# Expert 0's input: the last two chunks' rows picked by one-hot products, the other rows read early

## The chip, the cores and the metric

The kernel runs on one core of a Trainium2 chip. The metric is the device time of one execution in microseconds (us); every position in this text is counted from the start of the span of one profiled execution. The engines are PE (TensorE: matmuls and transposes, with its weight loads), DVE (VectorE), ACT (ScalarE), POOL (GpSimd) and SP (SyncE, which here only issues DMAs, in order). Each engine works through its own list in program order.

## The reference, cut to what matters

Three stages follow each other. A recurrence over 768 steps (2 batches, 8 heads, 48 x 48 states) gives `y`; a mixture of 8 experts, of which each token takes one, works on the 1536 tokens of width 384; a gated product works on its result.

```python
x = y.transpose(0, 2, 1, 3).reshape(1536, 384)
logits = x @ w_gate                       # 8 experts
expert_idx = argmax(logits, axis=1)
for i in range(1536):                     # place of a token in its expert's list
    e = expert_idx[i]
    if counts[e] < capacity:
        disp[e, counts[e]] = x[i]; pos[i] = counts[e]; counts[e] += 1; keep[i] = True
h = maximum(einsum('ecd,edf->ecf', disp, w1), 0)      # 384 -> 1024
y = einsum('ecf,efd->ecd', h, w2)                     # 1024 -> 384
out[i] = gate_w[i] * y[expert_idx[i], pos[i]]         # for kept tokens
result = ((out @ w_a) * (out @ w_b)) @ w_out          # 384 -> 1536 -> 384
```

## The kernel before

The order of all instructions is the order in which the Python code emits them (`manual_schedule`); nothing is moved by a scheduler. Waits follow from data and from buffers that are used again. Four parts stand one behind the other.

**Running products.** 96 steps of a scan on DVE, with norms on ACT; the change does not touch them.

**Chunks** (`for c in range(NC)`, 8 chunks of 96 steps, both batches at once). For a chunk, `scores` and `state_mm`/`state_dve` are followed by `outputs(c, b)`, which leaves `y` for batch `b`. `route_a` turns it into token rows `Ys[c]` (96 tokens x 384) and logits `LT`; `route_b` picks the expert (`OH`, a one-hot of 8) and adds to the running counts `EX`; `route_c` ranks the tokens by small products with a triangle and with ones, adds 1536 x expert, and has the slot of every token in `SLU`. Two indirect DMAs of POOL per chunk then write the 96 rows of a batch to their slots in `xs`, a table in DRAM of 8 x 1536 rows that was filled with zeros where experts read (`SLOT` = 240 rows each). The routing of a chunk runs one or two chunks behind; in the last pass (`c == 7`) chunks 5, 6 and 7 are ranked one after the other, chunk 7 one batch at a time.

**Experts.** 32 passes `i` = (expert `e`, quarter `fp`). `load_x(e)` reads 240 rows of `xs` into `R` (SP's queue); it waits for the scatters. `expert_x(e)` transposes them on PE and splits them into a rounded part (ACT) and a rest (DVE), the tile `XTT`. `hmm` has 18 matmuls per pass, `ymm` 18 more, one pass later. In a pass stand also: `wsplit(e + 1, fp)`, a quarter of the next expert's weights into a rounded part (ACT) and a rest (DVE, tile `whl`); `hl`, the rest of the hidden layer (DVE). Weights come by `wload` in 1.5 MB pieces into two buffers (tag `S`), so a piece can be loaded when the splits of the piece two before it are done. The table `UE` says in which expert a unit `n` of the third stage's weights is converted (`raw_load`, `conv_tt`, five DVE operations into a tile `cvt`); `store()` writes finished units to DRAM, in the first pass of the next expert that has units, right behind `wload(e + 1, 1)` on SP. `R`, `hh`, `hl`, `raw` and `cvt` share the nine buffers of tag `T`, and PSUM's tag `h` has three buffers.

Ahead of the first pass the split of the third and fourth quarter of expert 0's weights runs side by side with `tables()` (prefix sums of the counts and the table that takes a slot back to its token). 16 matmuls on ones (`busy`) stand on PE ahead of `expert_x(0)`; nothing reads their result.

**Gated product.** Weights converted while it runs, then rows scattered to the output. It is not touched.

Of the kernel before, what the change touches and what calls it, by code (L numbers as in the profile page):

```python
# [7 lines left out]
I32 = mybir.dt.int32  # L8
# [32 lines left out]
def body(tc, q, k, v, a_re, a_im, w_gate, w1, w2, cap, w_a, w_b, w_o, out, dbg=None):  # L41
# [59 lines left out]
    off_i = cpool.tile([1, E], I32, name="off_i")  # L101
    flag_i = cpool.tile([1, 1], I32, name="flag_i")

    xs = dp.tile([E * NT, DM], F32, name="xs")
    meta = dp.tile([NT, 2], I32, name="meta")
    wf = dp.tile([3, 128, DF], F32, name="wf")
    kid = dp.tile([CH, 128, GD], F32, name="kid")
# [272 lines left out]
    def run(g):  # L380
        for _ in g:
            pass
# [34 lines left out]
    for p in range(NP):  # L417
        if p == 2:
            zt = tT([SP, CU2], F32, "zt")
            V.memset(zt, 0.0)  # L420
            zfill = nc.gpsimd.dma_start(xs.rearrange("(a r) d -> a r d", a=E)[:, :SLOT].rearrange("a (p r) d -> p a (r d)", p=SP), zt.unsqueeze(1).to_broadcast([SP, 8, CU2]))

        if 0 < p < NP - 2:
            load_a(p + 2)
        if p < NP - 1:
            load_k(p)
        gens = []
        load_q(p)
        if p > 0:
            kinv_pre(p - 1, 1)  # L430
        if p + 1 < NP:
            if p == 0:
                gens.append(iter(range(8)))
            if p > 1:
                gens.append(qmul(p - 2))
            gens.append(norm_dve(p + 1))
        else:
            gens.append(qmul(p - 2))
            gens.append(iter(range(8)))
            KL[p] = KLb[p % 2]  # L440
            kl = tT([128, WP], F32, "kl")
            nc.sync.dma_start(kl, lrow(k, p * JP))
            lq = [tT([128, 16 * D], F32, f"last{i}") for i in range(4)]
            last = [kinv_last(8 * h, 8 * h + 8, lq[2 * h], lq[2 * h + 1], kl[:, h * 8 * D:(h + 1) * 8 * D]) for h in range(2)]
        if p > 0:
            if p < NP - 1:
                gens.append(iter(range(4 if p == 1 else 0)))
            gens.append(kinv_dve(p - 1))
        if p == NP - 1:
            QT = [tH([GD, 64, CH], F32, "QT0"), None]  # L450
        bg = chain(*gens)
        for i in range(JP):
            cm = cum(p * JP + i)
            next(cm)
            if p > 0 or i > 3:
                next(bg, None)
            next(cm)
            if p == 0 and i < 4:
                if i == 3:
                    for _ in range(3):  # L460
                        next(first[1])
                    V.tensor_add(g_t, *nx_t[1])
                    run(first[1])
                    norm_pre(1)
                    load_a(2)
                continue
            next(bg, None)
            if p > 0 and i == 2:
                kinv_exp(p - 1)
            if p > 1 and i == (4 if p < NP - 1 else 4):  # L470
                kinv_post(p - 2)
            if p == 0 and i == 5:
                norm_sq(2)
            if p == 0 and i == 9:
                m2_t = tT([128, JP * D], F32, "m2_t")
                V.tensor_add(m2_t, *nx_t[0])
            if i == (6 if p > 0 else 9) and p + 2 < NP:
                norm_pre(p + 2, m2_t)
            if i == 10 and p < NP - 1:
                kinv_pre(p, 0)  # L480
            if p == NP - 1:
                if i == 11:
                    QT[1] = tH([GD, 64, CH], F32, "QT1")
                for ii, pp, hf in CUTS:
                    if ii == i:
                        half(pp, hf)
            if p == NP - 1 and i == 9:
                bg = chain(bg, zip2(last[0], qmul(p - 1)))
            if p == NP - 1 and i == 13:
                kinv_post(p - 1)  # L490
        if p < NP - 1:
            run(bg)
# [167 lines left out]
    def route_c(c, b0=0, b1=B):  # L660
# [15 lines left out]
        pm = cpool.tile([CH, B], F32, tag="pm", name="slot", bufs=2)  # L676
        V.tensor_reduce(pm[:, :n], pri[:, :n], AX.X, ALU.add)
        yield
        V.tensor_copy(SLU[:, t2], pm[:, :n])
        for b in range(b0, b1):  # L680
            i = G.indirect_dma_start(out=xs[:], out_offset=bass.IndirectOffsetOnAxis(ap=SLU[:, B * c + b:B * c + b + 1], axis=0), in_=Ys[c][:, b].rearrange("t p d -> t (p d)"), in_offset=None)
            apart(i, xs_sc)
            after(i, [zfill])
            xs_sc.append(i)
            G.memset(gap_t, 0.0)
# [107 lines left out]
            V.tensor_tensor(lo, t, hi.bitcast(F32), ALU.subtract)  # L793
            yield

    xTs = {}
    cv = tS([128, 2, 4 * CU], I32, "cv0")
    u0 = units[0]
    NU0 = 3
# [5 lines left out]
    for c in range(NC):  # L805
# [5 lines left out]
        if c < NC - 1:  # L811
            scores(c + 1, 0)
            scores(c + 1, 1)
            next(st, None)
            if c > 0:
                route_a(c - 1)
            scores(c + 1, 2)
            scores(c + 1, 3)
            if c == NC - 2:
                run(st)  # L820
            run(zip2(route_b(c - 1) if c > 0 else iter(()), st))
            outputs(c, 0)
            if c + 1 < NC - 1:
                state_mm(c + 1, 0)
            outputs(c, 1)
        else:
            outputs(c, 0)
            run(route_c(c - 2))
            route_a(c - 1)
            run(route_b(c - 1))  # L830
            outputs(c, 1)
            run(route_c(c - 1))
            route_a(c, 0, 1)
            run(route_b(c, 0, 1))
            route_a(c, 1, 2)
            run(zip2(route_b(c, 1, 2), route_c(c, 0, 1)))
            run(route_c(c, 1, 2))
        if c + 1 < NC - 1:
            if c > 3:
                run(route_c(c - 1))  # L840
            state_mm(c + 1, 1)
# [19 lines left out]
        yield from conv_g(u0[n][0], 0, u0[n][1], x[:, :CU], x[:, CU:])  # L861
        conv_out(*u0[n], x[:, CU:].bitcast(F32))

    raw_load(NU0)
    V.tensor_tensor(EX[:, NC], EX[:, NC - 1], OH[:, NTAU - B:], ALU.add)
    tq.release()
    hp.release()

# [8 lines left out]
    for d in range(KD):  # L877
        for i in range(2):
            G.memset(x2[d][i].bitcast(F32), 0.0)
    XT, Hp, yps = {}, {}, {}  # L880
    offs = {}

    sel = xpool.tile([CH, NTAU, E], F32, name="sel")
# [82 lines left out]
        V.tensor_tensor(flag_i, nm[:, 0:1], nm[:, 1:2], ALU.max)  # L966
        yield

    Rt = {}

    def load_x(e):
        R = Rt[e] = tT([SP, 2, DM], F32, f"R{e}")
        after(nc.sync.dma_start(R, xs[e * NT:e * NT + SLOT].rearrange("(a p) d -> p a d", p=SP)), xs_sc)

    def expert_x(e):
        R = Rt[e]
        xp = [pse([128, KD, SP], f"xp{e}_{a}", f"xp{a}", 1) for a in range(2)]
# [42 lines left out]

    seq = [(e, fp) for e in range(E) for fp in range(4)]

    UE = {0: (3,), 1: (4, 5), 2: (6, 7), 3: (8,), 4: (9,), 5: (10,), 6: (11,)}
    load_x(0)
    wload(1, 0)
    side = chain(wsplit_g(0, 2, 4), wsplit_g(0, 3, 4))
    tb = tables()
    run(zip2(side, (next(tb) for _ in range(7))))


    busy = pse([128, 512], "busy", "y0", 1)
    for _ in range(16):
        PE.matmul(busy, ones_b, ones_b.unsqueeze(1).to_broadcast([128, 4, 128]), start=True, stop=True)
    XTT = tC([128, 2, 2, KD, SLOT], F32R, "XTT")
    expert_x(0)
    YPS = [pse([128, 2, SLOT], f"yps{d}", f"y{d}", 1) for d in range(KD)]
    def load_off(e):
        offs[e] = nc.values_load(off_i[:, e:e + 1], engines=[mybir.EngineType.Activation, mybir.EngineType.DVE], min_val=0, max_val=NT, skip_runtime_bounds_check_because="exclusive prefix sums of counts that add up to NT")
# [1 line left out]
    for i, (e, fp) in enumerate(seq):  # L1040
# [8 lines left out]
            m2load(i - 26)  # L1049
        hmm(e, fp)  # L1050
        if i == 0:
            next(tb)
        if i == 6:
            run(tb)
        if fp == 2:
# [17 lines left out]
            next(cg)  # L1073
        elif us and fp == 3:
            run(cg)
        if e + 1 < E:
            wsplit(e + 1, fp)
        elif fp < 2:
            m2split(fp)
# [257 lines left out]
```

## Time and profile before

| | |
|---|---|
| median of 3 runs | 619.63 us (617.08 to 622.54) |
| the profiled execution | 618.06 us, span 616.4 us |
| busy share of the span | PE 84%, DVE 71%, ACT 45%, POOL 13% |
| mean granted TensorE clock | 0.929 |
| chain that ended last | PE 63%, DVE 24%, DMA 6%, ACT 3% |

The shares are averages over stages with different limits. The chain of waits says, followed back from the last instruction, what each step waited for; it is read here for the stretch from the last chunk (from 212 us) to the fifth expert (326 us). Behind 326 us PE is busy without a gap until the last rows are written. [...]

### The profile page before, as it was taken

Reading aid. Unit: us, or ns where it says so; the run is one execution under the profiler, and the core shown is the slowest. Engines: PE = TensorE matmul, PEld = TensorE weight load, DVE = VectorE, ACT = ScalarE, POOL = GpSimd, SP = SyncE. Lnnn points to the kernel's source line nnn. Section 1 sums busy time; section 2 is a strip of 40 time slices with the busy share of each in tenths; the row PEclk is TensorE's granted clock in tenths of the full one; section 3 lists DMA queues with packets and bytes.
Section 4 is the critical chain, followed back from the end, with each engine's and each line's share of the span. In section 5 each row is a group of like instructions: output and inputs, shape, how many; then the busy total and the mean of one; then the engine's idle time right before and its main releaser. Section 6 shows DMA issues by size and latency. Waiting matters only on the chain.

```text
span 616.4 us, 10343 instructions
## 1 busy us (share of the span) xinstructions
PE 519.3 (84%) x4021; PEld 463.1 (75%) x4021; DVE 436.3 (71%) x951; ACT 276.1 (45%) x481; POOL 79.6 (13%) x127
## 2 busy tenths in 40 slices
PE   0064745789899888987999999999999999999993
PEld 0022422689889758987899999888888888888992
DVE  5899999975998853896688774766676777623331
ACT  5656563683435434553566563353443333211220
POOL 2000000040224273011221200000000000002121
PEclk9987677769999877997999999999999999999997
DMA  4148743289965127758578744121212121001010
GB/s 149 55 141 219 222 114 85 60 152 221 223 191 206 46 70 242 233 190 281 177 254 247 236 159 127 52 78 51 78 52 77 53 77 53 1 2 52 23 54 30
DMA packets 62945, 77.56 MB, mean 126 GB/s; under 512 B 29416, under 2 KB 52584, under 8 KB 62888
## 3 DMA queue, kind: packets, MB, share of 16 engines
q1 hardware_dynamic: 60040, 68.75, 37.8%
q0 software_dynamic: 2576, 7.68, 4.4%
q8 instruction: 33, 0.54, 0.4%
q10 hardware_dynamic: 272, 0.39, 0.2%
q14 instruction: 24, 0.20, 0.1%
HBM read 61.27 MB, written 15.54 MB: 125 GB/s over the span
## 4 chain that ended last, share of the span: by engine, by line
PE 63%; DVE 24%; DMA 6%; ACT 3%; issue 2%; SPq 0%; POOL 0%; POOLq 0%; DVEq 0%; ACTq 0%
PE ab L1102 24%; PE o L1118 12%; PE yps L1015 9%; PE h L999 8%; DVE t L271 4%; DVE A L273 3%; DMA wf<-cvt 2%; PE sc L581 2%; DVE KL L336 2%; PE l L299 1%; DMA temps<-in_a_re_dram 1%; DVE whl L711 1%; PE U L550 1%; PE xt L636 1%; DVE A L377 1%
## 5 line engine op out<-in xcount | busy, mean ns | idle before, releaser
L1102 PE MATMUL ab<-x2h,m2h 128*128 128x512 f32 (+1 forms) x480 | 142.1, 369 | 0.0
L1102 PEld LDWEIGHTS ab<-x2h,m2h 128*128 128x128 f32 x480 | 87.4, 188 | 14.4
L1102 PE MATMUL ab<-x2l,m2h 128*128 128x512 f32 (+1 forms) x240 | 88.8, 370 | 0.0
L311 PE MATMUL n<-temps,ident 128*128 128x384 f32 x40 | 27.9, 869 | 54.5 <-ACT temps L308 54.5
L1118 PE MATMUL o<-m2h,gh 128*128 128x384 f32 x288 | 73.6, 336 | 0.0
L999 PE MATMUL h<-XTT,whl 128*128 128x240 f32 x576 | 73.0, 282 | 0.5 <-ACT XTT L987 0.5
L1015 PE MATMUL yps<-hh,whl 128*128 128x240 f32 x384 | 72.0, 280 | 0.7 <-DVE x2l L1019 0.7
L999 PEld LDWEIGHTS h<-XTT,whl 128*128 128x128 f32 x576 | 69.9, 196 | 0.9 <-ACT XTT L987 0.9
L711 DVE TENSOR_TENSOR whl<-wr,whl 128x1536 fp32r<-128x1536 f32 (+1 forms) x38 | 57.1, 1502 | 14.1 <-ACT whl L707 14.0
L311 PEld LDWEIGHTS n<-temps,ident 128*128 128x128 f32 x40 | 12.1, 327 | 67.4 <-issue 38.8
L1015 PEld LDWEIGHTS yps<-hh,whl 128*128 128x128 f32 x384 | 61.9, 194 | 1.0 <-DVE x2l L1019 0.9
L1109 DVE TENSOR_TENSOR g<-ab,g 128x512 f32<-128x512 f32 (+1 forms) x40 | 25.5, 638 | 45.9 <-PE ab L1102 45.9
L1015 PE MATMUL yps<-hl,whl 128*128 128x240 f32 x192 | 53.9, 281 | 2.2 <-DVE hl L1004 2.2
L1118 PEld LDWEIGHTS o<-m2h,gh 128*128 128x128 f32 x288 | 52.5, 188 | 2.4
L1102 PEld LDWEIGHTS ab<-x2l,m2h 128*128 128x128 f32 x240 | 45.2, 188 | 6.9
L1118 PE MATMUL o<-m2h,gl 128*128 128x384 f32 x144 | 48.5, 337 | 0.0
L1110 ACT CAST gh<-g 128x512 fp32r<-128x512 f32 (+1 forms) x40 | 23.1, 578 | 55.6 <-DVE g L1109 55.6
L707 ACT CAST whl<-wr 128x1536 fp32r<-128x1536 f32 x32 | 47.3, 1480 | 0.5 <-DMA wr<-in_moe_w_dram 0.5
L1111 DVE TENSOR_TENSOR gl<-g,gh 128x512 fp32r<-128x512 f32 (+1 forms) x40 | 25.6, 639 | 25.8 <-ACT gh L1110 25.8
L1136 POOL DMA_INDIRECT out_dram<-acc,MT x12 | 11.7, 971 | 244.7 <-DVE acc L1134 243.1
L1015 PEld LDWEIGHTS yps<-hl,whl 128*128 128x128 f32 x192 | 37.2, 194 | 2.6 <-DVE hl L1004 2.6
L1108 ACT COPY g<-ab 128x512 f32<-128x512 f32 (+1 forms) x40 | 21.6, 541 | 29.5 <-PE ab L1102 29.5
(231 smaller groups left out, 950.4 us busy)
## 6 DMA issues: line engine op xcount, KB each, us to landing
wr<-in_moe_w_dram SPq DMA_DIRECT2D x16, 1536.0 KB
KN<-kid SPq DMA_DIRECT2D x7, 672.0 KB
kid<-KL SPq DMA_DIRECT2D x5, 896.0 KB
cv<-in_moe_w_a_dram SPq DMA_DIRECT2D x11, 384.0 KB
cv<-in_moe_w_b_dram SPq DMA_DIRECT2D x8, 384.0 KB
cv<-in_moe_w_out_dram SPq DMA_DIRECT2D x8, 384.0 KB
xs<-zt POOLq DMA_DIRECT2D x1, 2880.0 KB, 18.9
R<-xs SPq DMA_DIRECT2D x8, 360.0 KB
```

The source lines that it names most:

```text
L271: V.tensor_tensor(t, P, w, ALU.mult)
L311: PE.matmul(n2, ident, sq[:, :, c], start=(c == 0), stop=(c == 1))
L707: A.copy(hl[:, 0, sl], WR[w, e][:, hf])
L711: V.tensor_tensor(hl[:, 1, x], WR[w, e][:, hf, i * n:(i + 1) * n], hl[:, 0, x].bitcast(F32), ALU.subtract)
L999: PE.matmul(hp[:, f2], W[:, a, kk, f * 128:(f + 1) * 128], XT[e][:, b, kk], start=(i == 0), stop=(i == 3 * KD - 1))
L1015: PE.matmul(yps[e][d], W[:, a, f, d * 128:(d + 1) * 128], Hp[e, fp][b][:, f2], start=(f == 0 and i == 0), stop=(f == KF - 1 and i == 2))
L1102: PE.matmul(p, W[:, a].rearrange("p (k f) -> p k f", k=KD)[:, kk, (f % 4) * 128:(f % 4 + 1) * 128], x2[kk][b][:, c0:c0 + n], start=(i == 0 ...
L1108: A.copy(g, ps[0])
L1109: V.tensor_tensor(g, ps[1], g, ALU.mult)
L1110: A.copy(gh, g)
L1111: V.tensor_tensor(gl, g, gh.bitcast(F32), ALU.subtract)
L1118: PE.matmul(ops[s4], g[a][:, s4 * 128:(s4 + 1) * 128], W[:, b, f % 4], start=(f % 4 == 0 and i == 0), stop=(f % 4 == 3 and i == 2))
```

## The change

Expert 0 no longer reads all its rows from `xs`. `load_x(0)` is issued when only chunks 0 to 5 are scattered (in the last pass of the chunks, whose `route_c(5)` now stands first). The rows of chunks 6 and 7 that go to expert 0 are added to that by matrix products: `route_c` builds for each of these chunks and batches a one-hot `P0` (96 tokens x 240 slots, slot number equal to the token's slot) on DVE, and `x0_late` multiplies the token rows with it, three products of 128 x 240 in float32, accumulated over the four pairs in three banks of PSUM. `x0_rows` transposes what was read early, `x0_sum` adds both and leaves `XTT`. A late row of expert 0 is scattered to a spare part of `xs` (a ninth block, offsets `SLX`), so it does not touch what `load_x(0)` reads; the other late rows go where they went.

The 16 matmuls on ones are gone. `tables()` moves behind the first `hmm`, the split of expert 0's fourth quarter into pass 0, and expert 1's quarters into passes 1 to 3 of expert 0 as (none), (0), (1, 2), (3). Unit 3 is converted in expert 1 and every later pair one unit lower, so that expert 3 now has two units: experts 0 to 6 have 0, 2, 2, 2, 1, 1, 1 in place of 1, 2, 2, 1, 1, 1, 1.

```diff
@@ -101,7 +101,7 @@
...
-    xs = dp.tile([E * NT, DM], F32, name="xs")
+    xs = dp.tile([(E + 1) * NT, DM], F32, name="xs")
@@ -676,10 +676,24 @@
         pm = cpool.tile([CH, B], F32, tag="pm", name="slot", bufs=2)
...
         yield
-        V.tensor_copy(SLU[:, t2], pm[:, :n])
+        late = c >= NC - NL
+        if late:
+            if b0 == 0:
+                P0[c] = tT([CH, B, SLOT], F32, f"P0_{c}")
+            for b in range(n):
+                V.tensor_tensor(P0[c][:, b0 + b], slot_f, pm[:, b:b + 1].to_broadcast([CH, SLOT]), ALU.is_equal)
+            V.tensor_copy(SLU[:, t2], pm[:, :n])
+            V.tensor_scalar(pri[:, :n, 0], pm[:, :n], float(NT), float(E * NT), ALU.is_lt, ALU.mult)
+            V.tensor_tensor(SLX[:, t2], pm[:, :n], pri[:, :n, 0], ALU.add)
+        else:
+            V.tensor_copy(SLU[:, t2], pm[:, :n])
         for b in range(b0, b1):
-            i = G.indirect_dma_start(out=xs[:], out_offset=bass.IndirectOffsetOnAxis(ap=SLU[:, B * c + b:B * c + b + 1], axis=0), in_=Ys[c][:, b].rearrange("t p d -> t (p d)"), in_offset=None)
+            i = G.indirect_dma_start(out=xs[:], out_offset=bass.IndirectOffsetOnAxis(ap=(SLX if late else SLU)[:, B * c + b:B * c + b + 1], axis=0), in_=Ys[c][:, b].rearrange("t p d -> t (p d)"), in_offset=None)
             apart(i, xs_sc)
+            if late:
+                apart(i, x0_ld)
             after(i, [zfill])
@@ -793,7 +807,50 @@
             V.tensor_tensor(lo, t, hi.bitcast(F32), ALU.subtract)
...
-    xTs = {}
+    NL = 2
+    P0 = {}
+    lp = tc.alloc_tile_pool(name="late", bufs=1)
+    SLX = lp.tile([CH, NTAU], U32, name="SLX")
+    islot = tT([CH, SLOT], I32, "islot")
+    G.iota(islot, pattern=[[1, SLOT]], base=0, channel_multiplier=0)
+    slot_f = lp.tile([CH, SLOT], F32, name="slot_f")
+    A.copy(slot_f, islot)
+    x0_ld = []
+    Rt, XT = {}, {}
+    def load_x(e):
+        R = Rt[e] = tT([SP, 2, DM], F32, f"R{e}")
+        i = nc.sync.dma_start(R, xs[e * NT:e * NT + SLOT].rearrange("(a p) d -> p a d", p=SP))
+        after(i, xs_sc)
+        if e == 0:
+            x0_ld.append(i)
+    x0 = {}
+    def x0_rows():
+        x0["r"] = tT([128, KD, SLOT], F32, "x0r")
+        for a in range(2):
+            xp = ps1([128, KD, SP], f"xp0_{a}", "m")
+            for kk in range(KD):
+                PE.transpose(xp[:, kk], Rt[0][:, a, kk * 128:(kk + 1) * 128], ident[:SP, :SP])
+            A.copy(x0["r"][:, :, a * SP:(a + 1) * SP], xp)
+    def x0_late(c, b):
+        if not "z" in x0:
+            x0["z"] = [ps1([128, SLOT], f"xz{kk}", "nnm"[kk]) for kk in range(KD)]
+        y = Ys[c][:, b].rearrange("t p d -> t (p d)")
+        for kk in range(KD):
+            PE.matmul(x0["z"][kk], y[:, kk * 128:(kk + 1) * 128], P0[c][:, b], start=(c == NC - NL and b == 0), stop=(c == NC - 1 and b == B - 1))
+    def x0_sum():
+        X, r = XT[0], x0["r"]
+        for kk in range(KD):
+            V.tensor_tensor(r[:, kk], r[:, kk], x0["z"][kk], ALU.add)
+            A.copy(X[:, 0, kk], r[:, kk])
+        for kk in range(KD):
+            V.tensor_tensor(X[:, 1, kk], r[:, kk], X[:, 0, kk].bitcast(F32), ALU.subtract)
     cv = tS([128, 2, 4 * CU], I32, "cv0")
@@ -824,17 +881,23 @@
                 state_mm(c + 1, 0)
...
         else:
+            run(route_c(c - 2))
+            load_x(0)
+            route_a(c - 1)
             outputs(c, 0)
-            run(route_c(c - 2))
-            route_a(c - 1)
             run(route_b(c - 1))
...
             route_a(c, 0, 1)
+            x0_late(c - 1, 0)
             run(route_b(c, 0, 1))
             route_a(c, 1, 2)
+            x0_late(c - 1, 1)
             run(zip2(route_b(c, 1, 2), route_c(c, 0, 1)))
+            x0_rows()
+            x0_late(c, 0)
             run(route_c(c, 1, 2))
+            x0_late(c, 1)
         if c + 1 < NC - 1:
@@ -861,8 +924,11 @@
...
-    raw_load(NU0)
+    XTT = tC([128, 2, 2, KD, SLOT], F32R, "XTT")
+    XT[0] = XTT[:, 0]
+    x0_sum()
...
+    lp.release()
@@ -1020,19 +1080,10 @@
...
-    UE = {0: (3,), 1: (4, 5), 2: (6, 7), 3: (8,), 4: (9,), 5: (10,), 6: (11,)}
-    load_x(0)
+    UE = {1: (3, 4), 2: (5, 6), 3: (7, 8), 4: (9,), 5: (10,), 6: (11,)}
     wload(1, 0)
-    side = chain(wsplit_g(0, 2, 4), wsplit_g(0, 3, 4))
+    run(wsplit_g(0, 2, 4))
     tb = tables()
-    run(zip2(side, (next(tb) for _ in range(7))))
-    busy = pse([128, 512], "busy", "y0", 1)
-    for _ in range(16):
-        PE.matmul(busy, ones_b, ones_b.unsqueeze(1).to_broadcast([128, 4, 128]), start=True, stop=True)
-    XTT = tC([128, 2, 2, KD, SLOT], F32R, "XTT")
-    expert_x(0)
     YPS = [pse([128, 2, SLOT], f"yps{d}", f"y{d}", 1) for d in range(KD)]
@@ -1049,7 +1100,9 @@
             m2load(i - 26)
...
         if i == 0:
-            next(tb)
+            for _ in range(8):
+                next(tb)
+            wsplit(0, 3)
         if i == 6:
@@ -1073,7 +1126,10 @@
             next(cg)
...
             run(cg)
-        if e + 1 < E:
+        if e == 0:
+            for n in ((), (0,), (1, 2), (3,))[fp]:
+                wsplit(1, n)
+        elif e + 1 < E:
             wsplit(e + 1, fp)
```

On PE, this is what stood between the last routing step and expert 0's first matmuls before (`rk` is the rank of a chunk's tokens, `xp` the transposed rows, `h` the hidden layer of expert and pass):

```order
L1033 MATMUL busy_2334<-ones_b_79 128x512
L980 MATMUL xp0_0_2352<-ident_65,R0_2298 128x120 [waits DMAHW4_49]
L980 MATMUL xp0_0_2352<-ident_65,R0_2298 128x120 x2
L980 MATMUL xp0_1_2353<-ident_65,R0_2298 128x120 x3
L999 MATMUL h0_0_2371<-XTT_2351,whl0_0_1883 128x240 [waits Activation_49]
L999 MATMUL h0_0_2371<-XTT_2351,whl0_0_1883 128x240 x5
L999 MATMUL h0_0_2371<-XTT_2351,whl0_0_1883 128x240 [waits DVE_49]
L999 MATMUL h0_0_2371<-XTT_2351,whl0_0_1883 128x240 x11
```

and this is what stands around the transposes of the early rows now, with the rank of chunk 7's second batch behind them (`xz` are the three accumulating banks):

```order
L672 LDWEIGHTS ones_b_79
L672 MATMUL rk7_0_2265<-base_b_86,ones_b_79 96x8
L836 MATMUL xp0_0_2285<-ident_65,R0_2149 128x120 [waits DMAHW3_49]
L836 MATMUL xp0_0_2285<-ident_65,R0_2149 128x120 x2
L836 MATMUL xp0_1_2290<-ident_65,R0_2149 128x120 [waits Activation_49]
L836 MATMUL xp0_1_2290<-ident_65,R0_2149 128x120 x2
L844 MATMUL xz0_2240<-P0_7_2276,Y7_2232 128x240 [waits DVE_49]
L844 MATMUL xz1_2241<-P0_7_2276,Y7_2232 128x240
L844 MATMUL xz2_2242<-P0_7_2276,Y7_2232 128x240
L667 LDWEIGHTS tri_81
L667 MATMUL rk7_1_2298<-OH_98,tri_81 96x8 [waits DVE_49]
```

The transposes, which wait for the read of `R0`, now stand ahead of the last rank and not behind 16 products on ones; chunk 7's products stand between.

On SP, the DMAs from the last chunk on before (`R` rows of an expert, `wr0_1` the first layer of expert 1, `wr1_1` its second):

```order
L723 DMA raw3_2269<-in_moe2_w_a_dram 128x3x256 [waits DVE_49,DMAHW3_49,PE_49,Pool_49]
L973 DMA R0_2298<-xs_104 120x2x384 [waits DMASW3_49,DMASW2_49,DMASW4_49,DMASW1_49,DMASW5_49,DMASW0_49,DMASW6_49,DVE_49,DMASW7_49,PE_49,Pool_49]
L694 DMA wr0_1_2300<-in_moe_w1_dram 128x3x1024 [waits DMAHW5_49,DMAHW0_49,DVE_49]
L973 DMA R1_2367<-xs_104 120x2x384 [waits DMAHW6_49,DVE_49,PE_49]
L694 DMA wr1_1_2369<-in_moe_w2_dram 128x8x384 [waits DMAHW1_49,DVE_49,Activation_49]
```

and now:

```order
L824 DMA R0_2149<-xs_104 120x2x384 [waits DMASW3_49,DMASW4_49,DMASW2_49,DMASW5_49,DMASW1_49,DMASW6_49,DMASW0_49,DMASW7_49,DVE_49,DMAHW3_49,PE_49,Pool_49]
L708 DMA wr0_1_2355<-in_moe_w1_dram 128x3x1024 [waits DMAHW0_49,DVE_49]
L824 DMA R1_2366<-xs_104 120x2x384 [waits DMASW6_49,DMASW7_49,DMASW5_49,DMAHW5_49,DMASW0_49,Activation_49]
L708 DMA wr1_1_2368<-in_moe_w2_dram 128x8x384 [waits DMAHW6_49,DMAHW1_49,DVE_49]
L708 DMA wr0_2_2473<-in_moe_w1_dram 128x3x1024 [waits DMAHW4_49,DVE_49]
```

Expert 0's read and the first weights of expert 1 moved ahead of the last two chunks' scatters; for those waits now `R1`, and the second weights behind it.

On DVE, expert 3 from its second `whl` split to the first `hl` of expert 4, before (`hl3_2` is the rest of the hidden layer of expert 3, pass 2; `cvt8` is unit 8):

```order
L711 TENSOR_TENSOR whl0_4_3088<-wr0_4_2922,whl0_4_3088 128x1536 [waits Activation_49]
L1004 SCALAR_TENSOR_TENSOR hl3_2_3168<-h3_2_3148,hh3_2_3167 128x480 [waits Activation_49]
L1038 TENSOR_LOAD off_i_102
L734 TENSOR_SCALAR cvt8_3193<-raw8_3086 128x384 [waits DMAHW2_49]
L736 SCALAR_TENSOR_TENSOR cvt8_3193<-raw8_3086,cvt8_3193 128x384 [waits DVE_49]
L738 TENSOR_SCALAR cvt8_3193<-raw8_3086 128x384
L711 TENSOR_TENSOR whl1_4_3198<-wr1_4_3034,whl1_4_3198 128x1536 [waits DMAHW7_49,Activation_49]
L1004 SCALAR_TENSOR_TENSOR hl3_3_3221<-h3_3_3201,hh3_3_3220 128x480 [waits Activation_49]
L740 TENSOR_TENSOR cvt8_3193<-cvt8_3193 128x384 [waits DVE_49]
L742 SCALAR_TENSOR_TENSOR cvt8_3193<-raw8_3086,cvt8_3193 128x384 [waits DVE_49]
L711 TENSOR_TENSOR whl1_4_3198<-wr1_4_3034,whl1_4_3198 128x1536 [waits Activation_49]
L1004 SCALAR_TENSOR_TENSOR hl4_0_3270<-h4_0_3250,hh4_0_3269 128x480 [waits Activation_49]
```

and the corresponding rows now, from the third operation of unit 7 on:

```order
L752 TENSOR_SCALAR cvt7_3209<-raw7_3100 128x384
L754 TENSOR_TENSOR cvt7_3209<-cvt7_3209 128x384 [waits DVE_49]
L756 SCALAR_TENSOR_TENSOR cvt7_3209<-raw7_3100,cvt7_3209 128x384 [waits DVE_49,Activation_49]
L725 TENSOR_TENSOR whl1_4_3216<-wr1_4_3048,whl1_4_3216 128x1536 [waits DMAHW5_49,Activation_49]
L1064 SCALAR_TENSOR_TENSOR hl3_3_3239<-h3_3_3219,hh3_3_3238 128x480 [waits DMAHW4_49,Activation_49]
L748 TENSOR_SCALAR cvt8_3260<-raw8_3158 128x384 [waits DMAHW1_49,DVE_49]
L750 SCALAR_TENSOR_TENSOR cvt8_3260<-raw8_3158,cvt8_3260 128x384 [waits DVE_49]
L752 TENSOR_SCALAR cvt8_3260<-raw8_3158 128x384
L754 TENSOR_TENSOR cvt8_3260<-cvt8_3260 128x384 [waits DVE_49]
L756 SCALAR_TENSOR_TENSOR cvt8_3260<-raw8_3158,cvt8_3260 128x384 [waits DVE_49,Activation_49]
L725 TENSOR_TENSOR whl1_4_3216<-wr1_4_3048,whl1_4_3216 128x1536 [waits Activation_49]
L1064 SCALAR_TENSOR_TENSOR hl4_0_3293<-h4_0_3273,hh4_0_3292 128x480 [waits DMAHW7_49,DVE_49,Activation_49]
```

Seven operations more stand ahead of the `whl` split that releases the buffer for expert 5's weights, and with it the stores of units 7 and 8 behind them on SP.

## Rows read from the trace of the kernel before

**Rows 1.** The chain of waits, 211 to 244 us: start us, length us, what.
```profile
211.73 0.48 PE y L624 x4
...
223.32 0.17 PE rk L667
...
223.99 0.17 DVE slot L677
...
225.13 4.00 DMA xs<-Y,SLU
...
229.31 3.50 DMA R<-xs
...
234.87 6.33 PE h L999 x36
...
243.84 2.02 PE h L999 x18
```
**Rows 2.** The timeline of the last chunk: start us, us, engine, line, operation.
```profile
212.59 0.16 DVE L644 TENSOR_TENSOR EX<-EX,OH 96x16 bf16<-96x16 bf16 x1
...
214.65 3.09 PE L636 MATMUL xt<-IW,ytile 112*96 112x104 f32 x16
...
215.61 0.92 POOL L681 DMA_INDIRECT xs<-Y,SLU  x1 [7.70 <-DVE SLU L679]
...
220.02 1.75 PE L636 MATMUL xt<-IW,ytile 112*96 112x104 f32 x16
...
224.79 0.28 DVE L893 TENSOR_TENSOR sel<-LT,MX 96x128 f32<-96x128 f32 x1
...
227.49 0.55 DVE L711 TENSOR_TENSOR whl<-wr,whl 128x384 fp32r<-128x384 f32 x1
```
**Rows 3.** Windows of 2 us: PE, PEld, DVE, ACT, POOL busy; PEclk, DMA share, GB/s.
```profile
212.00:214.00 2.00, 2.00 (x28) 1.81 (x24) 0.65 (x5) 0.00 (x0) 0.00 (x0) 0.50 0.00 0
...
224.00:226.00 2.00, 1.45 (x10) 0.81 (x11) 1.97 (x9) 0.92 (x3) 1.78 (x3) 0.88 0.50 148
...
232.00:234.00 2.00, 1.15 (x6) 1.09 (x6) 0.00 (x0) 0.20 (x1) 2.00 (x3) 0.59 1.01 377
...
306.00:308.00 2.00, 1.93 (x17) 1.93 (x18) 2.00 (x4) 0.47 (x1) 0.80 (x1) 1.00 0.02 5
```
**Rows 4.** Waits of PE, 200 to 616 us: us in total, times, longest us.
```profile
PE xp L980 <- DMA R<-xs: 2.8, 1, 2.8
...
PE fp L962 <- DVE XTT L989: 3.2, 1, 3.2
...
PE yps L1015 <- DVE hl L1004: 1.4, 1, 1.4
```
**Rows 5.** The chain of waits, 276 to 323 us, experts 2 to 4.
```profile
276.12 7.42 DMA wf<-cvt
...
284.97 4.13 PE yps L1015 x18
289.09 2.70 PE h L999 x18
...
297.70 7.57 DMA wf<-cvt
...
320.98 2.02 PE h L999 x18
```
**Rows 6.** The timeline of DVE, 293 to 317 us.
```profile
293.12 0.34 DVE L734 TENSOR_SCALAR cvt<-raw 128x384 int32<-128x384 int32 x1
...
295.50 1.75 DVE L711 TENSOR_TENSOR whl<-wr,whl 128x1536 fp32r<-128x1536 f32 x1
...
311.51 1.76 DVE L711 TENSOR_TENSOR whl<-wr,whl 128x1536 fp32r<-128x1536 f32 x1 [1.14 <-ACT whl L707]
...
313.19 0.65 DVE L1004 SCALAR_TENSOR_TENSOR hl<-h,hh 128x480 fp32r<-128x480 f32 x1
...
314.82 1.75 DVE L711 TENSOR_TENSOR whl<-wr,whl 128x1536 fp32r<-128x1536 f32 x1
```

More of the change, by code (lines that the diff above doesn't have):

```diff
@@ L420, in body @@
             V.memset(zt, 0.0)
-            zfill = nc.gpsimd.dma_start(xs.rearrange("(a r) d -> a r d", a=E)[:, :SLOT].rearrange("a (p r) d -> p a (r d)", p=SP), zt.unsqueeze(1).to_broadcast([SP, 8, CU2]))
+            zfill = nc.gpsimd.dma_start(xs.rearrange("(a r) d -> a r d", a=E + 1)[:E, :SLOT].rearrange("a (p r) d -> p a (r d)", p=SP), zt.unsqueeze(1).to_broadcast([SP, 8, CU2]))
         if 0 < p < NP - 2:
@@ L879, in body @@
             G.memset(x2[d][i].bitcast(F32), 0.0)
-    XT, Hp, yps = {}, {}, {}
+    Hp, yps = {}, {}
     offs = {}
@@ L967, in bounds @@
         yield
[L969 to L973, printed above, removed]
     def expert_x(e):
```

## Prediction

> **What bounds the kernel now.** I read the chain of waits first, from the last chunk on. Between the last slot (`slot`, done at 224.2) and expert 0's first `h` at 234.87 it runs through little but data movement [rows 1]: the last scatter lands 4.2 us behind POOL's start at 225.13, the read of `R0` takes 3.5, the transposes and the rounding copy the 2.1 that are left. PE waits 2.8 us for `R0` [rows 4]. Then I read the clock by windows [rows 3]. It is 0.50 from 212 on, is back when the last logits take 1.75 us instead of 3.09 [rows 2], and falls within 232 to 234 (0.59), in or right behind the wait for `R0`. So the first 36 matmuls of `h` take 6.33 us, where 18 take 2.02 at the full clock: 2.3 us more than they need.
>
> The rest of the experts is read for what happens to a gain made there. Their passes take 2.02 + 2.02 us on PE and are interrupted twice, in the first half of experts 2 and 3. Both times the chain goes through a store `wf<-cvt` that takes 7.42 and 7.57 us [rows 5], as it stands behind 1.5 MB of weights on SP; the buffer of that `cvt` is the one that the next `hl` gets. The first time PE stands still for 3.2 us and the clock falls (18 matmuls in 4.13, the next 18 in 2.70); the second time it stands 1.4 us and the clock stays [rows 4, 5].
>
> **The change part by part.** Positions are those of the profiled execution of before.
>
> *Early read.* Rank 5 now stands first in the last chunk, so PE waits there until `EX` is ready (212.59 + 0.16) where it began with `outputs` at 211.73 [rows 1, 2]. All chunk work on PE comes 1.0 us later by this. The scatters of chunk 5 come 1.4 us earlier, as the rank no longer stands behind `outputs`: POOL's first start moves from 215.61 to about 214.3 [rows 2], the second follows 1.2 later. With 4.2 for landing and 3.5 for the read [rows 1], `R0` is there at about 223.2.
>
> *One-hot products.* A product of 104 columns in float32 is two rows of the profile; 16 take 3.09 us at the half clock [rows 2], so 1.5 at the full one, and three products of 240 columns take 1.5 / 16 x 6 x 240 / 104 = 1.3 us, twice that at the half clock. There are four such groups: 5.2 us on PE. A one-hot of 96 x 240 on DVE lies between 0.28 for 96 x 128 and 0.55 for 128 x 384 [rows 2]: 0.4.
>
> *Path to the first `h`.* Rows 2 have chunk 7's first logits at 220.02; 1.0 later is 221.0. Then PE works: logits 0.9, group (6, 0) 1.3, logits 0.9, group (6, 1) 1.3, rank of batch 0 0.5 (223.32 to `slot`'s first step [rows 1]): 225.9. DVE needs three steps of 0.17 to the slot and 0.4 for the one-hot: 226.8. Meanwhile PE transposes `R0`, in two parts that share a bank, with a copy between, 1.2 us of the 2.1 above as the clock is full: 227.1; and `R0` has 2.7 us in hand. Group (7, 0) 228.4, rank 228.9, slot and one-hot 229.7, group (7, 1) 231.0. The last add (0.4) and copy end near 231.7, the first two a third of a microsecond each ahead of it, and `h` starts at 231.4: **3.5 us earlier** than 234.87.
>
> *What then is late.* Pass (0, 1) needs a third PSUM buffer of tag `h`; the first is free when DVE has made `hl0_0`, and ahead of that stand four pieces of `whl` (0.55 each [rows 2]) which wait for an ACT cast that starts after the last copy (231.7 + 1.5). That gives 235.4, and `hl` (0.65 [rows 6]) 236.1. PE ends pass (0, 0) and the small products of `tables()` at 234.3, so it stands still for 1.8 us. Were the clock full, pass (0, 2) starts at 236.1 + 2.0 + 2.0 + 0.7 = 240.8, where before has 243.84 [rows 1]: 3.05 gained. `sel`, the first step of `tables()`, waits for the last scatters, as its pool lies where `SLX` lay; they land at 230.4 + 4.2 = 234.6, ahead of `hl0_0`, so this wait costs nothing (and 1 us for each us that they land after 236). `R1` lands 3.5 later, 2 us before PE wants it.
>
> *DVE.* What DVE did while PE ran on ones now lies beside expert 0: nine steps of `tables()` at 0.28 or less [rows 2], 2.4 us, and a whole split of 1.75. The split frees the buffer for the second weights of expert 1, so these are issued only at 240.3. If they land after the 7.4 us of a store behind such a load, ACT's cast and with it `hl0_3` come 1.3 us late; if 1.3 earlier, not at all. I take the middle: **the gain at the end of expert 0 is 2.5 us** (1.8 to 3.1). The spare block of `xs`, the offsets `SLX` and the iota cost PE nothing.
>
> *Expert 3.* Experts 1 and 2 keep two units each, and the order of rows and waits there is that of before: both stops stay, as I find no wait that is gone. Expert 3 has now two units, and the first `hl` to reuse a `cvt` buffer there is `hl4_1`. A conversion costs DVE 2.4 us (293.12 to 295.50); 1.1 of it fits where DVE waited for ACT (311.51), so the last split ends not at 314.82 + 1.75 = 316.6 but at 317.9 [rows 6]. SP then issues the weights and 0.4 later the stores, 318.25, and the first lands at 325.8 [7.5 as in rows 5]. `hl4_1` ends at 326.4. PE has ended pass (4, 2) at 320.98 + 2.02 [rows 5], plus some 0.4 since expert 3's last rests, which free the output banks, are late as well: 323.4, and has one product to do. It stands still for about 2.8 us, 3.2 with the 0.4. The nearest row for what the clock does is the wait for `R0`, 2.8, in which it fell [rows 3, 4]; a fall costs 4.13 + 2.70 - 2 x 2.02 = 2.8 [rows 5]. So **this third stop costs 6.0 us** (1.5, if it is like the second stop; 6.0, if like the first). Behind it PE has no gaps in which a delay would vanish.
>
> [...]
>
> *Sum.* 618.06 - 2.5 + 6.0 = 621.6 for an execution like the profiled one. The median of before stands 1.6 above the profiled one, so the forecast for the median is **623 us**: a gain of 3 us at the start, given back with interest at a new stop 80 us later. A measurement of this kernel tells about 1% (6 us) from no change, so this counts as no change.
>
> **The rivals.**
>
> *The third stop is short* (0.20). It is if the store lands 6 rather than 7.5 us after its issue, or if DVE wins back the 1.3. Then it costs 1.5 as in rows 4, the clock stays, and the time is 619.6 - 2.5 + 1.5 = 618.6. For it: expert 3's ACT is less loaded than I count. Against: both stores of rows 5 agree within 2%.
>
> *Slower: the clock falls in expert 0* (0.15). [...]
>
> *Faster: the first stop loses its fall of the clock* (0.14). The store of unit 3 and the wait of a `raw` load for it are gone from expert 1's part of SP's queue. If that brings the stores of the first stop forward by 1.5 us, it falls from 3.2 to under 2 and saves 1.5 + 2.8, and if expert 3's stop is short too: 619.6 - 3.1 - 4.3 + 0.5 = 612.7. Against: those stores wait for DVE's last split of expert 2's weights, not for the queue.
>
> *It doesn't do what it says* (0.08): `R0` lands late, since its scatters or the read take longer with the 1.5 MB of weights right behind them. The transposes stand ahead of the last rank, so each us after 225.9 goes straight to `h`; with 3 us the start gains nothing, 619.6 + 6.0 = 625.6.
>
> **How the numbers follow.** The forecast has 0.43. Faster by over 1% is the third rival, 0.14. Slower by over 1% takes most of the second, half of the last and the tail of the forecast: 0.16. The rest, 0.70, is within 1%. The range leaves out most of the fast rival and the tail of the slow ones: 615 to 627.5.
>
> **What would show it.** Right: `h` of expert 0 starts 3 to 4 us earlier, no wait of PE for `R`, a stop of PE for `hl` near the second pass of expert 4 beside those of experts 2 and 3, and a granted clock of 0.5 behind it. Wrong: no stop in expert 4 (then the time is under 617), a half clock between 236 and 243, or PE waiting for `R0` or for a slot's one-hot longer than 0.9 us. The forecast fails first on the third stop, which is worked out from an order and two stores, and then on the clock.

## The result and the profile after

Over 20 runs each, the changed kernel takes 626.32 us at the median (620.38 to 631.27), the kernel before 617.95 (614.20 to 625.12); the ratio is 1.0116 (95% interval 1.0093 to 1.0139). So it is slower by about 7 us. The ratio is taken over the fast executions alone, so it is not the quotient of the two medians. The profiled execution takes 626.74 us, span 625.0.

The two profiled executions are not level ahead of the change: from the first loads on, all of the changed kernel's scan lies about 2 us later, over the same instructions. In the profiled executions of the ten further kernels below this step starts anywhere from 210.15 to 214.52 us, whichever kernel they come from, so the shift does not belong to the change. So lengths are counted here from a common point, the start of the scan's last step on DVE (`S`, at 210.72 us before and at 212.28 after; 1.56 apart). From there to the end of the span before has 405.7 us and after 412.7: 7.0 more, which is what the ratio says.

The waits of PE from 200 to 350 us, which answer [rows 4] (us in total, times, longest us):

```profile
PE yps L1075 <- DVE hl L1064: 6.8, 4, 4.1
PE fp L1028 <- DVE XTT L1049: 3.1, 1, 3.1
...
PE h L1059 <- DVE hl L1064: 1.2, 1, 1.2
PE xz L844 <- DVE P L686: 0.9, 1, 0.9
```

PE's wait for `R` is gone, and the stop of 3.1 us in expert 2 (`fp`) is still there. The first line holds four waits: 0.8 in each of experts 0 and 1, 1.1 in expert 3, and a new one of 4.1 in expert 4. The kernel before has two of these four: over the window that [rows 4] names its waits for `hl` are 2.2 us in all, 0.8 in expert 1 and the 1.4 in expert 3 that the row shows alone. The windows of 2 us (busy PE, PEld, DVE, ACT, POOL; then granted clock, DMA share, GB/s) answer [rows 3]:

```profile
228.00:230.00 2.00, 2.00 (x14) 1.75 (x14) 0.14 (x2) 0.46 (x1) 1.01 (x2) 1.00 0.02 7
230.00:232.00 2.00, 1.12 (x3) 0.99 (x4) 1.01 (x6) 0.00 (x0) 0.09 (x1) 0.65 0.25 74
...
234.00:236.00 2.00, 1.76 (x8) 1.79 (x9) 1.19 (x6) 1.77 (x2) 2.00 (x3) 0.50 0.20 15
...
330.00:332.00 2.00, 2.00 (x11) 2.00 (x11) 2.00 (x3) 0.00 (x0) 0.00 (x0) 0.50 0.04 9
```

The clock is 1.00 through the first of chunk 7's two groups of products. It falls within 230 to 232 (0.65), in the wait of 0.9 us for the last one-hot, and stays low through the last group and expert 0's first pass (0.50 in 234 to 236). It falls again behind the new stop (0.50 in 330 to 332). The chain of waits shows both places (start us, us, what):

```profile
230.88 2.78 PE xz L844 x6
...
234.24 3.77 PE h L1059 x18
...
240.08 2.00 DVE off_i L996
...
243.15 1.68 DVE whl L725
244.84 6.62 DMA wr<-in_moe_w_dram
...
254.76 0.58 DVE hl L1064
255.34 0.04 issue
255.38 2.18 PE yps L1075 x17
...
277.64 7.32 DMA wf<-cvt
...
319.58 8.85 DMA wf<-cvt
...
328.52 0.67 DVE hl L1064
329.18 0.04 issue
329.23 3.68 PE yps L1075 x17
332.91 2.13 PE h L1059 x18
```

The last group of one-hot products takes 2.78 us, the one ahead of it 1.22; the first pass 3.77 where a pass has 2.02. Then stands something that [rows 2] did not prepare for: a cast of eight numbers, `off_i`, takes 2.00 us. All of the chain to 255.34 hangs on it, as the split behind it frees the buffer for `wr1_1`. The timeline beside it (start us, us, engine, line, operation):

```profile
238.91 1.62 POOL L945 MEMSET x2h<- 128x1776 f32 x1
240.08 2.00 DVE L996 CAST off_i<-inc 1x8 int32<-1x8 f32 x1
240.43 1.62 POOL L945 MEMSET x2l<- 128x1776 f32 x1
```

The cast ends at 242.08, POOL's last memset at 242.05. In the kernel before the cast took 0.15 us, and the memsets began behind it:

```profile
226.63 0.15 DVE L930 CAST off_i<-inc 1x8 int32<-1x8 f32 x1
...
227.53 1.59 POOL L879 MEMSET x2h<- 128x1776 f32 x1
```

The gain can be followed along PE's passes, always from the scan's last step. The first `h` comes 2.2 us earlier than before (21.96 against 24.15). At pass (0, 2) it is 1.0, at the second pass of expert 1 nothing is left (45.1 in both). From expert 1 to the end of expert 4 the changed kernel loses 6.5 us: 0.3 won at the second stop, 0.8 lost ahead of pass (4, 2), where PE now waits shortly for `x2l`, and 6.0 at the new stop. Behind it the distance stays; 0.6 is added by the last write.

### The profile page after: what moved, and what is told of

Its sections match the earlier page's. It is cut to its first block, busy times and chain, and to the rows that moved or that the text cites. A ratio compares the mean times of both kernels' runs of the same rounds, so it can differ in the third digit from the quotient of the medians.

```text
span 625.0 us, 10389 instructions
## 1 busy us (share of the span) xinstructions
PE 521.7 (83%) x4029; PEld 467.5 (75%) x4029; DVE 441.0 (71%) x962; ACT 277.5 (44%) x485; POOL 77.1 (12%) x128
## 4 chain that ended last, share of the span: by engine, by line
PE 58%; DVE 27%; DMA 7%; ACT 3%; issue 2%; SPq 0%; DVEq 0%; POOLq 0%; POOL 0%; ACTq 0%
PE ab L1158 24%; PE o L1174 12%; PE yps L1075 6%; PE h L1059 6%; DVE t L271 4%; DMA wf<-cvt 4%; DVE A L273 3%; DVE whl L725 2%; PE sc L581 2%; DVE KL L336 2%; PE l L299 1%; DMA temps<-in_a_re_dram 1%; DMA temps<-in_a_im_dram 1%; PE U L550 1%; DVE A L377 1%
## 5 line engine op out<-in xcount | busy, mean ns | idle before, releaser
L1075 PE MATMUL yps<-hh,whl 128*128 128x240 f32 x384 | 73.6, 284 | 1.3 <-DVE x2l L1079 1.3
L1158 PEld LDWEIGHTS ab<-x2l,m2h 128*128 128x128 f32 x240 | 45.2, 188 | 6.9
```

What stands on the lines that cost most here:

```text
L1075: PE.matmul(yps[e][d], W[:, a, f, d * 128:(d + 1) * 128], Hp[e, fp][b][:, f2], start=(f == 0 and i == 0), stop=(f == KF - 1 and i == 2))
L1158: PE.matmul(p, W[:, a].rearrange("p (k f) -> p k f", k=KD)[:, kk, (f % 4) * 128:(f % 4 + 1) * 128], x2[kk][b][:, c0:c0 + n], start=(i == 0 ...
```

## The experiments

Theory A says that the time is lost at the new stop, which comes from expert 3's second unit and a store behind weights, and that the early start was lost to the clock; theory E, formed after e4, adds the cast that POOL's memsets hold up. Their rivals stand with each run. Ratios are against runs of before on the same chip. Their medians were 619.3 to 619.5 for e1 to e10 and 617.95 for the changed kernel, so a difference of 1 to 2 us between the medians of two rows says little. "To expert 1" is the time from the scan's last step to the second pass of expert 1, "to the end" to the end of the span, both in the profiled execution. One execution is not the median: e6's and e10's are the fastest of their 12, 4.6 and 3.5 us under their medians. So the lengths show where time goes, and the ratios how much. The profiled execution of e2 lay 6 us over its own median, so no lengths are given for it.

| kernel | median us | ratio to before (95%) | to expert 1 | to the end |
|---|---|---|---|---|
| before | 617.95 | 1 | 45.1 | 405.7 |
| the changed kernel | 626.32 | 1.0116 (1.0093 to 1.0139) | 45.1 | 412.7 |
| e1 unit 3 back in expert 0 | 621.25 | 1.0064 (1.0029 to 1.0099) | 44.0 | 404.4 |
| e2 before, new table of units | 623.05 | 1.0064 (1.0023 to 1.0104) | | |
| e3 stores first | 615.39 | 0.9940 (0.9906 to 0.9974) | 45.6 | 398.9 |
| e4 filled stops | 625.81 | 1.0127 (1.0074 to 1.0180) | 45.2 | 412.5 |
| e5 offsets by subtraction | 622.50 | 1.0052 (1.0012 to 1.0092) | 44.5 | 410.2 |
| e6 filled stops and subtraction | 622.25 | 1.0056 (1.0026 to 1.0086) | 40.6 | 405.4 |
| e7 before, stores first | 613.05 | 0.9916 (0.9882 to 0.9951) | 43.1 | 396.9 |
| e8 e3 and e6 together but for e4's last products, `nps` moved | 610.02 | 0.9862 (0.9821 to 0.9902) | 41.9 | 395.6 |
| e9 memsets later | 622.52 | 1.0051 (1.0018 to 1.0084) | 41.8 | 409.2 |
| e10 e6 with unit 3 back | 619.70 | 1.0006 (0.9979 to 1.0034) | 41.6 | 404.4 |

### The new stop in expert 4: e1, e2

```diff
+    raw_load(NU0)
...
-    UE = {1: (3, 4), 2: (5, 6), 3: (7, 8), 4: (9,), 5: (10,), 6: (11,)}
+    UE = {0: (3,), 1: (4, 5), 2: (6, 7), 3: (8,), 4: (9,), 5: (10,), 6: (11,)}
```

> The changed kernel (626.3, ratio 1.0116) with the old table of units: unit 3 is converted in expert 0 again, so expert 3 has one unit. Theory A (the stop in expert 4, 4.1 us and a fall of the clock, comes from expert 3's second unit and costs 6.0): no wait of PE for hl over 1 us in expert 4, the clock stays 1.00 from 300 us on, and the time falls by 6.0, given back in part by the 2.4 us of conversion that DVE gets in expert 0: 620 to 622.5. Rival B (experts 0 and 1 are late from the moved splits and tables, and the stop in expert 4 follows from that lateness): the stop stays, 625 to 628.

e2 is the reverse edit in the kernel before:

> The kernel before (618.0) with nothing but the new table of units: unit 3 in expert 1, two units in expert 3. Theory A: a third stop near the second pass of expert 4 with a half clock behind it, 6.0 us, less up to 1 us for the conversion that leaves expert 0: 623 to 624, ratio 1.008 to 1.010. Rival B: no third stop, 617 to 618.5.

e1 has no stop in expert 4, its clock is 1.00 from 300 us on, and it takes 621.25 us, as theory A has it. All that PE waits for in e1 from 300 us on is the old second stop:

```profile
PE yps L1076 <- DVE hl L1065: 1.3, 1, 1.3
```

In e2 the kernel before gets a third stop (3.5 us for `hl` in expert 4) with a clock of 0.50 behind it:

```profile
334.00:336.00 2.00, 2.00 (x12) 2.00 (x11) 1.97 (x4) 0.34 (x1) 1.47 (x1) 0.50 0.15 14
```

Its ratio is 1.0064, 4 us; A's 1.008 to 1.010 lies within the interval, the no change of rival B does not. So the stop in expert 4 comes from expert 3's second unit, in either kernel, and not from lateness at the start. What the table of units costs is 3 us by the ratios of the changed kernel and e1 (1.0116 and 1.0064), 5 by their medians, and 4 by the ratio of e2. That is less than the 6.0 of the new stop in the profiled execution. The expectations had it so: e1 gets 2.4 us of conversion back into expert 0, and e2 is freed of it there.

### What the stops wait for: e3, e7

```diff
             load_x(e + 1)
+            store()
             wload(e + 1, 1)
...
-        if fp == 0 and us:
-            store()
```

> The changed kernel with each store of finished units on SP ahead of the second weights of the next expert instead of right behind them. Theory A (hl waits for a store that stands behind 1.5 MB): the stores land in 2 to 3 us, the three stops in experts 2, 3 and 4 go, with the two falls of the clock: 626.3 - 6.0 - 1.1 - 6.0 = 613. Rival C (DVE is full in experts with two units, some 16.4 of 16.9 us by its rows, and the weights now land later): PE waits for DVE's splits or x2l instead, the clock falls somewhere all the same, 619 to 623.

The same edit in the kernel before:

> The kernel before with nothing but the stores ahead of the second weights. Theory A: its two stops go with the fall of the clock, 618 - 6.0 - 1.4 = 611, and it is 1 to 3 us faster than the changed kernel with the same edit (ratio 0.994), as that one has the gain of its early start lost to the clock and to the cast. Rival H (the early start is worth something once the stops are gone): as fast as that one or slower, 614 to 616.

The stores now stand on SP ahead of the 1.5 MB, as the first of them in e3 show (start us, us, what):

```profile
272.41 5.14 SPq L765 DMA_DIRECT2D wf<-cvt  x2
278.70 0.37 SPq L708 DMA_DIRECT2D wr<-in_moe_w_dram  x1
```

All three stops go in e3, and so do both in e7; the clock is 1.00 from 240 to 388 us in both. The waits of PE in e3 from 240 to 350 us:

```profile
PE yps L1075 <- DVE hl L1064: 1.6, 2, 0.9
PE h L1059 <- DVE hl L1064: 1.2, 1, 1.2
PE yps L1075 <- DVE x2l L1079: 1.1, 2, 0.7
```

615.4 is nearer to A's 613 than to C's 619 to 623: small waits for DVE are left, but nothing that halves the clock behind 240 us. With stores first, the kernel before is at 613.05, 2 us faster than the changed one with the same edit, as A expected, though the two intervals overlap and rival H is not excluded.

In the changed kernel, where the stores of 192 KB stand behind the 1.5 MB, the trace has 7.2 to 8.9 us for them. No row here has the time of a store ahead of the weights, and none shows what makes a store behind them take that long.

### The start of expert 0: e4, e5, e9, e6

e4 fills the places where PE waits with products on ones (2, 4, 3 and 8 of 128 x 512):

```diff
+            if a == 0:
+                warm(2)
...
-            run(route_c(c, 1, 2))
+            rc = route_c(c, 1, 2)
+            next(rc)
+            warm(4)
+            run(rc)
             x0_late(c, 1)
+            warm(3)
...
+            for _ in range(8):
+                PE.matmul(wb, ones_b, ones_b.unsqueeze(1).to_broadcast([128, 4, 128]), start=True, stop=True)
```

> The changed kernel with products on ones (2, 4, 3 and 8 of 128x512, results unused) in the four places where PE waits between chunk 7's ranks and the second pass of expert 0. Theory A (the start of expert 0 lost its gain to the clock, which fell to 0.5 at 230.6 in a wait of 0.9 us): the clock stays 1.00 from 221 on, the last group takes 1.2 instead of 2.8 us and the first pass 2.0 instead of 3.8; the second pass starts 2.5 to 3 us earlier and the time is 623 to 624. Rival D (the clock falls anyway, or the products on ones delay PE as much as they save): 626 to 627.

The clock held: 1.00 in each window from 220 to 238 us, of which one is shown; the first pass takes 2.1 us.

```profile
230.00:232.00 2.00, 1.90 (x13) 1.20 (x12) 1.83 (x7) 1.87 (x4) 2.00 (x3) 1.00 0.26 78
```

This is no chance of one execution. In all four kernels with these products (e4, e6, e8, e10) the clock is 1.00 from 224 to 252 us. In all five without them (the changed kernel, e1, e3, e5, e9) it falls, in three of them in the wait for the last one-hot or right behind it (0.65 in 230 to 232 in the changed kernel, 0.50 in 236 to 238 in e3), and in e1 and e9 only in the first pass of `h` (0.52 in 230 to 232 in e9).

Pass (0, 2) starts 2.2 us earlier in e4 than in the changed kernel (29.65 against 31.83). Yet the time is that of the changed kernel, so neither theory has both the clock and the time right. The cause is in DVE's timeline, beside POOL's:

```profile
235.89 4.20 DVE L1007 CAST off_i<-inc 1x8 int32<-1x8 f32 x1
...
236.93 1.61 POOL L956 MEMSET x2h<- 128x1776 f32 x1
238.45 1.61 POOL L956 MEMSET x2l<- 128x1776 f32 x1
```

The cast came earlier and waited longer, again to the end of POOL's last memset (240.06). Two tests of that. e5 changes the form of the step alone:

```diff
+        V.tensor_tensor(off_i, inc[0:1], n[0:1], ALU.subtract)
         V.tensor_sub(inc, inc, n)
         yield
-        V.tensor_copy(off_i, inc[0:1])
```

> The changed kernel with the eight offsets off_i written by a subtraction of two operands in place of a cast of one (same values). In the profile of the changed kernel that cast took 2.00 us where it took 0.15 before, and ended with POOL's last memset of x2 (240.43 + 1.62). Theory E (a DVE cast waits until POOL's run of memsets is over, a subtraction does not): the step takes under 0.3 us, wr1_1 is issued 1.9 us earlier against its own second pass, PE's wait for hl in the last pass of expert 0 (0.82) goes, the time falls by 1.1: 625. Rival F (DVE itself is blocked, whatever the form): the 2 us stay, 626.

e9 keeps the cast and changes when the memsets run:

```diff
-    for d in range(KD):
-        for i in range(2):
-            G.memset(x2[d][i].bitcast(F32), 0.0)
...
+            G.tensor_copy(gap_t, p2[0:1, 0:1])
+            for d in range(KD):
+                for x in x2[d]:
+                    G.memset(x.bitcast(F32), 0.0)
             wsplit(0, 3)
```

> The changed kernel with the cast of the offsets as it was, and POOL's six memsets of x2 held back until DVE has done the step two behind that cast. Theory E (the cast is held by POOL's memsets, not by its form as such): the cast takes 0.15 us, wr1_1 is issued 1.9 us earlier against its own second pass, and the wait of 0.8 in the last pass of expert 0 goes: 625. Rival I (the cast is slow in this place for another reason): 2 us, 626.

In e5 the subtraction runs in the middle of the memsets:

```profile
237.15 1.62 POOL L945 MEMSET x2h<- 128x1776 f32 x1
238.26 0.15 DVE L994 TENSOR_TENSOR off_i<-inc,n_e 1x8 int32<-1x8 f32 x1
238.67 1.62 POOL L945 MEMSET x2l<- 128x1776 f32 x1
```

In e9 the cast runs ahead of them:

```profile
235.83 0.16 DVE L993 CAST off_i<-inc 1x8 int32<-1x8 f32 x1
236.94 1.58 POOL L1105 MEMSET x2h<- 128x1776 f32 x1
```

Theory E holds in both, F and I fall; the wait in the last pass of expert 0 is gone in both. The kernel before shows the like in its first microseconds, where a DVE cast of 96 x 16 takes 2.23 us and ends with POOL's memsets:

```profile
2.59 2.23 DVE L86 CAST base_b<-ibase 96x16 bf16<-96x16 int32 x1 [1.55 <-POOL ibase L84]
...
4.22 0.56 POOL L152 MEMSET KL<- 128x256 f32 x2
```

Both times fell by 3.8 us where E expected 1.1 to 1.3. For e5 its one profiled execution has a place where more can come from: its stop in expert 4 is 2.9 us, not 4.1, and the clock behind it stays at 1.00, as the window shows in which the stop ends:

```profile
326.00:328.00 2.00, 1.64 (x14) 1.64 (x15) 2.00 (x4) 0.47 (x1) 0.92 (x1) 1.00 0.05 8
```

For e9 there is no such place: that execution has a stop of 3.9 with a fall (0.50 in 324 to 328), and was 2.5 us ahead at the first `h` already, for the clock fell later there. The surplus of e9 is not settled, and that of e5 rests on this one execution.

e6 has e4's and e5's edits together:

> The changed kernel with the filled stops, which held the clock but gave no time, and with the offsets by subtraction. In the run with filled stops alone the cast took 4.20 us, and two waits of PE for hl in expert 0 (1.15 and 1.51) took back what the clock had given. Theory E: both waits go, the second expert starts 2.7 us earlier against the end of the scan than in the changed kernel, the time is 623.5. Rival G (the first stop, in expert 2, ends by DVE's and the store's own chain, and takes up whatever was gained): PE waits longer there, 626.

Expert 1's second pass starts 4.5 us earlier than in the changed kernel (40.6 against 45.1), more than e4 and e5 give one by one (0 and 0.6), and the first stop is 2.7 us, not longer: up to here E holds. Its 622.25 is 1.3 under E's 623.5. But it is also what e5 takes without the products on ones (ratio 1.0052 against 1.0056), so the medians show nothing of the 3.9 us by which e6's trace is ahead of e5's at expert 1. Rival G had the first stop take up the gain, which this execution does not show. Its second stop did grow, to 3.2 us from the 1.1 of the changed kernel, with a fall of the clock behind it (0.50 in 302 to 304). Whether later stops take the gain in most executions is not shown.

### All together: e8, e10

> The changed kernel with stores ahead of the second weights, products on ones in three places up to the first pass, the offsets by subtraction, and nps in a PSUM bank of its own, so that the second pass needs no buffer that hl frees. Theory A with E: against stores first alone (615.4) the clock gives 3.2, the waits of 1.2 and 0.9 us in expert 0 go: 610 to 612, faster than the kernel before with stores first by at least 1. Rival C (DVE is full in experts 1 to 3): the gain of the start is waited away there, 613 to 615.

e8 also gives `nps`, the token counts of `tables()`, a PSUM bank apart from tag `h`:

```diff
-        nps = pse([CH, E], "nps", "h", 3)
+        nps = pse([CH, E], "nps", "xp0", 1)
```

e8 (with e3's and e5's edits and e4's first three groups of products) takes 610.02 us, the fastest of all: 1.4% under the kernel before, 3 us under e7, though the two intervals touch. From 240 to 350 us PE waits in all for

```profile
PE yps L1086 <- DVE hl L1075: 2.1, 2, 1.3
PE yps L1086 <- DVE x2l L1090: 1.0, 2, 0.7
```

> The changed kernel with filled stops, the offsets by subtraction and unit 3 in expert 0 again: the early read and the one-hot products without what the trace of the changed kernel showed to go against them (clock, cast, expert 3's second unit); stores stay behind the second weights. Theory A with E: no stop in expert 4, expert 1's second pass 4 us earlier against the end of the scan than in the kernel before, the first two stops stay: 614 to 616, ratio about 0.993. Rival J (unit 3's conversion, 2.4 us of DVE in expert 0, takes the gain): 618 to 620.

e10 reaches expert 1's second pass 3.5 us ahead of before, but takes 619.70: J's time, though not by J's means alone. PE waits 1.5 us for expert 2's rows, which the chain shows to be read for 9.44 us, issued 0.46 behind a piece of 1.5 MB:

```profile
247.46 0.37 SPq L708
...
247.92 9.44 DMA R<-xs
```

So with the stores where they were, another small transfer behind weights takes 1.5 us of the early start in this execution. It is still 1.3 shorter than before; the medians show no difference.

## Why the prediction was right, and where it was wrong

The time, 626.3 us, is inside the stated range, and the third stop was called. But the likeliest case was no change (623, +0.5%), and the kernel is slower by 1.2%, so the time lies near the upper end of a wide range and not at the forecast. The sum had 3.5 us more (6.0 less 2.5); the two profiled executions are 7.0 apart. Of the 3.5 that are missing 2.5 were lost at the start, the rest is the wait for `x2l` and the last write, less what the second stop gave. By the sum's own terms:

- **Early read: right.** Chunk 5's scatter starts at 215.71, which is 214.15 on the clock of before, where about 214.3 was forecast, and PE never waits for `R0`.
- **Start of `h`: 3.5 forecast, 2.2 measured.** The working had the last group of products at the full clock, 1.3 us. It ran at the half clock in 2.78, and that 1.5 is the difference. This term hangs on where the clock falls: in e1 and e9, where that group ran at the full clock, `h` starts 4.7 us earlier than before (19.45 from the scan's last step), in e3 and e5 1.9.
- **End of expert 0: 2.5 forecast, 0 measured. This is the step that failed.** The forecast took the clock as full from 231 on. That is the rival "the clock falls in expert 0" (0.15): it fell in the 0.9 us wait for the last one-hot (0.65 in 230 to 232). It cost 1.5 in the products and 1.75 in the first pass, 3.3 where a fall in expert 2 of the kernel before cost 2.8 [rows 5]; the kernels with and without products on ones show that it was the clock. Part of this fell into PE's wait for `hl0_0`, which became shorter than forecast (1.2 for 1.8): at pass (0, 2) 1.05 of the forecast 3.05 was left. That last 1.05 went to the load of `wr1_1`, where 0.55 was forecast to go. The forecast had it issued at 240.3 (241.9 here), it came at 244.84. The step "nine steps of `tables()` at 0.28 or less" took its prices from rows in which POOL was not at its memsets; one of them took 2.00. In the kernel before this stretch stood ahead of the memsets, and the change moved it into them. No rival had that, though the trace of before had a sign of it, the cast of 2.23 us shown above. e6 shows the same start with neither loss: 4.5 us ahead of before.
- **Third stop: 6.0 forecast, 6.0 measured**, with a longer wait (4.1 instead of 3.2, as the store took 8.85 us and not 7.5) and a cheaper fall (1.9 over 35 matmuls instead of 2.8). The lateness of expert 3's last rests, 0.4 in the forecast, was 0.8. e1, e2 and e3 show the cause that was given for it, two units and a store behind weights.
- **The other rivals.** The third stop can be short: in e6's execution it is 1.5 us and in e5's 2.9, and the clock stays in both (1.00 from 322 to 332 in e5). In e2, e4 and e9 it is 3.4 to 3.9 and the clock falls (0.50 behind it in e2 and e9). The first stop stayed at 3.1. `R0` was not late.

So the early read did what it was to do, 4.5 us at most at expert 1. The changed kernel had lost it 23 us behind the first `h`, and the table of units cost 6.0 more in the profiled execution, 3 to 5 by the times of e1 and e2.

## What to carry to other kernels

When steps are moved, look at what the neighbouring engines do in the new place, for each step and not for the sum of its durations: a 0.15 us cast became 2.0 and 4.2 us there. A gain on PE that leaves short waits in place of one filled with products can give itself back through the clock, as 3.3 us did here. Filling the new waits held the clock in all four kernels that had it (1.00 from 224 to 252 us). But e4 is no faster than the changed kernel for it, nor e6 than e5, and in e8, which is faster, it is one of several edits. So look at the waits behind the gain as well. And put small stores that free a buffer ahead of large prefetches on the same queue: here that was worth 5 us in the kernel before and 11 in the changed one, more than the early read.

## What the runs showed of the hardware

- Beside POOL's memsets the DVE cast of `off_i`, float32 to int32 of 1 x 8 elements, lasted to the end of the whole run of them: 2.00 us to the end of the second memset that it met (the changed kernel), 4.20 to the end of the third (e4); 0.15 (before) and 0.16 (e9) with none. A subtraction of two operands and a scan in the same stretch ran at 0.15 to 0.17, and a reduction of one operand to 96 x 16 at its 0.28 (e5), so one input alone did not make an operation wait. The cast did not get in between two memsets, so here the price was the run and not one memset. What holds the cast back is not shown.
- What PE did before the clock fell differs. In the experts the clock was 1.00 behind stops of 2.7 us (e6) and 2.9 (e5) and 0.50 behind stops of 3.0 (e10), 3.1 (e9) and 3.2 (before). Ahead of expert 0 it fell in a wait of 0.9 us that stood behind short ranks and a stop of 0.6 (the changed kernel). In the kernel before a fall behind a stop cost 2.8 us, so an edit that changes a stop a little can be worth more, or less, than its own term.
